# Sliding-window attention with a squared-ReLU feed-forward: two pairs of x, and whole q and k matrices, transposed by DMA

## The chip, the cores and the metric

The kernel runs on one core of one Trainium2 chip. The metric is the time of one execution on the device, in microseconds. Before the change it is 294.82 us (median of 3 runs, 294.8 to 296.04).

## What is computed

Attention over 8 batches, 8 heads, 576 positions and a head size of 64: each position sees itself and the 63 before it. The result, 4608 tokens of 512 values, goes through a feed-forward layer with the square of a ReLU.

```python
scores = np.matmul(q, k.transpose(0, 1, 3, 2)) / np.sqrt(D)
rel = pos[:, None] - pos[None, :]
attn = softmax(np.where((rel >= 0) & (rel < 64), scores, -1e9))
x = np.matmul(attn, v).transpose(0, 2, 1, 3).reshape(4608, 512)
h = np.maximum(x @ w_in, 0.0)          # 512 -> 2048
out = (h * h) @ w_out                  # 2048 -> 512
```

Inputs and output are float32; the products run on float16 copies.

## The kernel before, in words

The tokens are cut into nine blocks of 512. Blocks 0 to 7 hold the first 512 positions of a batch each; block 8 holds the last 64 positions of all batches and needs two k matrices (`k`, `k2`). A block has four pairs of heads (`hp` 0 to 3).

What happens to a block, by the function names in the code:

- **Load and cast.** `load_part` (line 193) loads q, k and v of a block in four pieces of 128 x 512 each from SyncE's queue, `cast_part` (206) makes float16 copies on GpSimd. The float32 pieces live in a ring of ten (`stp`), the float16 pieces of q and k in six buffers each (`p16p`, line 46). Blocks 0 to 2 are loaded by pairs of heads instead (`load_qk_pair`, `cast_qk_pair`).
- **Transposition of q and k.** `transpose_part` (225) lets a DMA from SyncE's queue transpose one piece of 128 x 512 into its quarter of `qT` or `kT`. Blocks 0 to 2 do this on TensorE (`T`, 236).
- **Scores.** `Sc` (263) multiplies for one pair of heads and applies the exponential on ScalarE (283); `M` (286) applies the mask on VectorE as a minimum. The probabilities `pm` live in a ring of four tiles.
- **Second product.** `AV` (293) multiplies with v, which has a column for the sum; `N` (310) divides by that sum on VectorE and writes `xs`, the 512 tokens x 128 values of the pair, in float16.
- **Transposition of x.** `X` (319) brings `xs` into `xT` (values on the partitions): four 128x128 transpositions on TensorE (332) into the pair's own PSUM bank, and one copy out of it, on ScalarE for the blocks here (334, shown as line 118 in the profile). Only block 8 uses a DMA transposition of 128 x 512 for each pair (324).
- **First layer.** `F1` (339) does four matmuls of 512 columns for one of 16 slices of 128 features; VectorE applies the ReLU (349), ScalarE the square (350). For block 8 `L1S` does it in seven products of half size.
- **Second layer.** `F2` for the first two blocks, then `L2S` (543), which forms the product from seven half-size products (`product`, 432, eight matmuls of 256 columns each); VectorE and ScalarE add the parts into `osb`, and `store` writes it from SyncE's queue.

The order is written out by hand. Each of the last eight steps (loop at line 800, step n) runs the second layer of block n and the first layer of block n+1 as a list `fill` of about 30 groups, and puts the attention of block n+2 between the groups: for the first two pairs the scores before group 8, masks before groups 11 and 12, `AV` and `N` before group 14, and `X` of the two pairs before groups 16 and 17; the other two pairs follow 11 groups later (lines 856 to 863; steps 1 and 2 differ by a few groups). Before each group `next_part` (732) is called as often as a quota says; each call issues one load and one cast, and one transposition of q or k whose load lies at least four parts back. SyncE works through its queue in this order: a DMA that waits for a cast holds up the loads and stores behind it.

Every engine takes its instructions in order. SyncE issues DMAs only, and its DMAs share eight completion counters in turn, so each waits for the eighth before it.

Of the kernel before, what the change touches and what calls it, by code (L numbers as in the profile page):

```python
# [9 lines left out]
FP16 = mybir.dt.float16  # L10
# [5 lines left out]
def kernel(  # L16
# [13 lines left out]
    nc = tc.nc  # L30
    B, H, S, D = q.shape
    NT, DM = out.shape
    DFF = moe_w_in.shape[1]
    P = 128
    HP = H // 2
    NBLK = B + 1
# [6 lines left out]

    const = ctx.enter_context(tc.tile_pool(name="const", bufs=1))
    stp = ctx.enter_context(tc.tile_pool(name="stp", bufs=10))
    p16p = ctx.enter_context(tc.tile_pool(name="p16p", bufs=6))
    vpool = ctx.enter_context(tc.tile_pool(name="vpool", bufs=2))
    tpool = ctx.enter_context(tc.tile_pool(name="tpool", bufs=5))
    apool = ctx.enter_context(tc.tile_pool(name="apool", bufs=2))
# [53 lines left out]
    st = {}  # L103
# [12 lines left out]
    def copy(engine, out, in_):  # L116
        if engine is nc.scalar:
            engine.activation(out=out, in_=in_, func=AF.Copy, scale=1.0)  # L118
        else:
            engine.tensor_copy(out=out, in_=in_)  # L120
# [23 lines left out]
        copy(engine, w_out_sb[:, f, :], st["w_out", f][:])  # L144


    p16 = {}
    ev, od, qT, kT = {}, {}, {}, {}

    def new_v(g, half=0):  # L150
        ev[g, half] = vpool.tile([P, 4, H, VW], FP16, name="v_ev", tag="ev", bufs=3)
        nc.gpsimd.memset(ev[g, half][:, :, :, D:VW], 1.0 / X_SCALE)
        if g < B:
            od[g] = vpool.tile([P, 3, H, VW], FP16, name="v_od", tag="od", bufs=2)
            nc.gpsimd.memset(od[g][:, :, :, D:VW], 1.0 / X_SCALE)

    def load_qk_pair(g, what, hp, queue=nc.sync):
        src = {"q": q, "k": k}[what]  # L160
        queue.dma_start(
            out=piece(what, g, hp)[:].rearrange("p (h x) -> p h x", h=2),
            in_=src[g, pair(hp), 0:512, :].rearrange("h (p i) d -> p h (i d)", i=4))
# [6 lines left out]
                in_=v[g, 2 * hp + hh, 0:512, :].rearrange("(c p) d -> p c d", p=P))  # L170

    def cast_qk_pair(g, what, hp, engine):
        t = p16p.tile([P, 512], FP16, name=f"{what}16", tag=f"{what}16")
        p16[what, g, hp] = t
        copy(engine, t[:].rearrange("p (i h d) -> p h i d", i=4, h=2),
             st[what, g, hp][:].rearrange("p (h i d) -> p h i d", i=4, h=2))

    def cast_v_pair(g, hp, engine):
# [27 lines left out]
    def cast_part(g, what, c):  # L206
        if what[0] == "v":
            half = 1 if what == "v2" else 0
            if (g, half) not in ev:
                new_v(g, half)  # L210
            copy(nc.gpsimd, ev[g, half][:, c, :, 0:D],
                 st[what, g, c][:].rearrange("p (h d) -> p h d", h=H))
            return
        t = p16p.tile([P, 512], FP16, name=f"{what}16", tag=f"{what[0]}16")
        p16[what, g, c] = t
        copy(nc.gpsimd, t[:], st[what, g, c][:])

    def shift_v_parts(g):
        for m in range(3):
# [5 lines left out]
    def transpose_part(g, what, c):  # L225
        to = {"q": qT, "k": kT, "k2": kT}[what]
        key = (g, 1 if what == "k2" else 0)
        if key not in to:
            to[key] = tpool.tile([P, HP, 512], FP16, name=f"{what}T", tag="T")
        nc.sync.dma_start_transpose(out=to[key][:, :, c * P:(c + 1) * P], in_=p16[what, g, c][:])  # L230


    pm, av, xs, xT = {}, {}, {}, {}
    at_ps = [ps_at.tile([P, 2, 512], FP32, name=f"at{i}") for i in range(2)]

    def T(g, hp, pool=ps_tr, tag="tr", engine=nc.scalar, own=None):
# [73 lines left out]
    def N(g, hp):  # L310
        a = av[g, hp][:, :, 0:4 * VW].rearrange("p h (j e) -> p h j e", e=VW)
        rden = apool.tile([P, 2, 4], FP32, name="rden", tag="rden")
        nc.vector.reciprocal(out=rden[:], in_=a[:, :, :, D])
        x = apool.tile([P, 4, 2, D], FP16, name="xs", tag="xs", bufs=3)
        xs[g, hp] = x
        nc.vector.tensor_tensor(out=x[:].rearrange("p j h d -> p h j d"), in0=a[:, :, :, 0:D],  # L316
                                in1=rden[:].unsqueeze(3).broadcast_to([P, 2, 4, D]), op=ALU.mult)

    def X(g, hp, engine=nc.scalar, pool=ps_tr, tag="tr", own=None):

        if g not in xT:
            xT[g] = xtpool.tile([P, DMC, 512], FP16, name="xT", tag="xT")
        if g == B:
            nc.sync.dma_start_transpose(out=xT[g][:, hp, :].rearrange("p (j t) -> p j t", j=4),
                                        in_=xs[g, hp][:].rearrange("p j h d -> p (j h d)"))
            return
        if own is not None:
            tr = at_ps[own][:, 0, :].bitcast(FP16).rearrange("p (a b) -> p a b", a=2)
        else:
            tr = pool.tile([P, 2, 512], FP16, name="xtr", tag=tag)  # L330
        for jp in range(4):
            nc.tensor.transpose(out=tr[:, 0, jp * P:(jp + 1) * P], in_=xs[g, hp][:, jp, :, :],  # L332
                                identity=ident[:])
        copy(engine, xT[g][:, hp, :], tr[:, 0, :])
# [265 lines left out]

    ORDER = (1, 2, 6, 5, 7, 3, 4)

    seq = list(range(NBLK))
    PARTS = {g: ("q", "k", "v") for g in range(B)}
    PARTS[B] = ("q", "k", "k2", "v", "v2")

    with tc.manual_schedule():
# [21 lines left out]
        new_v(g0)  # L629
        dve, pool, act = nc.vector, nc.gpsimd, nc.scalar  # L630
        cast_qk_pair(g0, "q", 0, dve)
        cast_qk_pair(g0, "k", 0, dve)
        cast_qk_pair(g0, "q", 1, pool)
        cast_qk_pair(g0, "k", 1, dve)
        cast_qk_pair(g0, "q", 2, pool)
# [20 lines left out]
        cast_v_pair(g0, 2, dve)  # L656
        AV(g0, 0)
        N(g0, 0)
        AV(g0, 1, 0)
        N(g0, 1)  # L660
        cast_v_pair(g0, 3, act)
        add_mask(g0, 3, True)
        Sc(g0, 3, True)
        AV(g0, 2)
        N(g0, 2)
        X(g0, 0)
        X(g0, 1, act, ps_f2, "f2")
        AV(g0, 3, 0)
        N(g0, 3)
        X(g0, 2)  # L670
        for i in range(4):
            for c in range(DMC):
# [59 lines left out]
        def next_part():  # L732

            if parts_left:
                g, w, c = parts_left.pop(0)
                load_part(g, w, c)
                cast_part(g, w, c)
                if w[0] != "v":
                    pending.append((g, w, c))
                elif g < B and c == 3:  # L740
                    shift_v_parts(g)
                behind = len(load_list) - len(parts_left) - 1
            else:
                behind = len(load_list) + 99
            while pending and behind - load_list.index(pending[0]) >= 4:
                transpose_part(*pending.pop(0))
# [53 lines left out]
        for n in range(1, NBLK):  # L800
            g = seq[n]
# [26 lines left out]
            a, b = iter(first), iter(second)  # L828
# [86 lines left out]
```

## Time and profile before

| | |
|---|---|
| median of 3 runs | 294.82 us |
| the profiled execution | 296.1 us |
| its span, first to last instruction | 294.3 us |
| granted TensorE clock | 1.0 |
| TensorE matmuls busy | 284.0 us (96%) |
| VectorE, ScalarE, GpSimd busy | 225.8, 176.8, 128.8 us |
| DMA transpositions of q, k, k2 from SyncE | 24, 24, 4 |
| of x from SyncE (block 8) | 4 |
| 128x128 transpositions of x on TensorE | 128 |

A row of the order of time has the start in us from the span's start, the duration, the engine, the line, the operation, the tiles written and read, and the shape; "x4" is a run of equal instructions, whose duration reaches from the first start to the last end. SPq is SyncE's queue: its durations are those of issuing, and "to landing" counts from the issue to the last byte. Matmuls are pipelined, so one instruction's duration is longer than the distance between two starts. A group's row has the count, the busy time and the mean ns of one, and then the idle time ahead of it and what ended it.

### The profile page before, as it was taken

How to read it: one execution, taken by the hardware profiler on the slowest of the kernel's cores; microseconds unless marked ns; L12 is line 12 of the kernel's file. 1: busy time of each engine (PE TensorE's matmuls, PEld its weight loads, DVE VectorE, ACT ScalarE, POOL GpSimd, SP SyncE). 2: the span in 40 equal slices, each digit the busy share in tenths (PEclk: the TensorE clock that was granted, in tenths of full speed). 3: DMA queues.
4: the chain of work that ended last, by engine and by line, in shares of the span. 5: the costliest groups of instructions: out<-in, count | busy, mean ns of one | idle time of the engine just before them, and what ended most of it. 6: DMA issues, size and time to landing. Idle time of an engine off the chain costs nothing.

```text
span 294.3 us, 7488 instructions
## 1 busy us (share of the span) xinstructions
PE 284.0 (96%) x2945; PEld 183.9 (62%) x2945; DVE 225.8 (77%) x396; ACT 176.8 (60%) x306; POOL 128.8 (44%) x216
## 2 busy tenths in 40 slices
PE   6789999999999999999999999999999999999994
PEld 5444445554445466667666766666666666888883
DVE  4868628698866887888769877987798889878781
ACT  3657847687376556565665566556564655687821
POOL 5778859955583366339226723832342000000002
PEclk9999999999999999999999999999999999999999
DMA  7999999979999998999899999899997024201015
GB/s 231 274 368 392 404 289 282 269 156 195 198 273 199 212 215 144 202 218 195 175 208 234 197 164 233 156 193 207 209 209 204 2 37 92 89 3 73 0 73 143
DMA packets 142627, 56.07 MB, mean 190 GB/s; under 512 B 127712, under 2 KB 134112, under 8 KB 142592
## 3 DMA queue, kind: packets, MB, share of 16 engines
q1 hardware_dynamic: 141120, 53.95, 85.8%
q10 hardware_dynamic: 1328, 1.25, 1.3%
q0 software_dynamic: 144, 0.39, 0.6%
q8 instruction: 23, 0.38, 0.6%
q14 instruction: 12, 0.10, 0.1%
HBM read 38.80 MB, written 9.44 MB: 164 GB/s over the span
## 4 chain that ended last, share of the span: by engine, by line
PE 91%; DMA 4%; SPq 1%; DVE 1%; ACT 1%; issue 0%; POOL 0%; DVEq 0%
PE hps L346 36%; PE chain L434 14%; PE side L434 12%; PE ops L382 5%; PE at L306 4%; PE at L468 4%; PE at L276 3%; PE side L382 2%; PE chain L382 2%; DMA hsum<-in_v_dram 2%; DMA w_st<-in_moe_w_in_dram 2%; PE more L434 2%; PE at L332 2%; PE at L434 1%; PE tr L245 1%; SPq L168 1%
## 5 line engine op out<-in xcount | busy, mean ns | idle before, releaser
L350 ACT ACTIVATE h<-hr 128x512 f16<-128x512 f32 x128 | 80.0, 630 | 78.6 <-DVE hr L349 78.6
L346 PE MATMUL hps<-xT,w_in_sb 128*128 128x512 f16 x496 | 122.5, 379 | 0.3 <-DVE hr L349 0.3
L349 DVE TENSOR_SCALAR hr<-hps 128x512 f32<-128x512 f32 x127 | 85.7, 686 | 32.0 <-PE hps L346 29.7
L346 PEld LDWEIGHTS <-w_in_sb 128*128 128x128 f16 x500 | 46.6, 98 | 42.6 <-issue 1.2
L434 PEld LDWEIGHTS <-hsum 128*128 128x128 f16 x448 | 43.0, 98 | 11.8
L120 POOL CAST v_ev<-st_v 128x512 f16<-128x512 f32 x29 | 22.2, 766 | 42.9 <-DMA st_v<-in_v_dram 42.9
L120 POOL CAST k<-st_k 128x512 f16<-128x512 f32 x33 | 23.0, 701 | 34.2 <-DMA st_k<-in_k_dram 31.6
L434 PEld LDWEIGHTS <-h 128*128 128x128 f16 x336 | 32.7, 98 | 8.5 <-issue 0.8
L283 ACT ACTIVATE pm<-at 128x1024 f16<-128x1024 f32 x35 | 34.1, 1013 | 4.0 <-PE at L276 4.0
L375 POOL DMA_DIRECT2D out_dram<-osb x3 | 1.8, 594 | 63.1 <-ACT osb L550 61.7
L316 DVE TENSOR_TENSOR xs<-at,rden 128x512 f16<-128x512 f32 x36 | 24.9, 691 | 1.2
L290 DVE TENSOR_TENSOR pm<-pm,mask 128x1024 f16<-128x1024 f16 x32 | 23.9, 759 | 1.9 <-ACT pm L283 1.9
L410 DVE TENSOR_TENSOR hsum<-h 128x1024 f16<-128x1024 f16 x28 | 21.0, 750 | 5.2 <-ACT h L350 5.0
L434 PE MATMUL chain<-wsum,hsum 128*128 128x256 f16 x192 | 24.9, 273 | 0.0
L221 POOL CAST v_od<-st_v 64x512 f16<-64x512 f32 x30 | 21.3, 711 | 1.6
L120 POOL CAST q<-st_q 128x512 f16<-128x512 f32 x25 | 17.5, 721 | 6.6 <-DMA st_q<-in_q_dram 6.3
L382 PEld LDWEIGHTS <-h 128*128 128x128 f16 x128 | 11.6, 98 | 12.2
L118 ACT ACTIVATE xT<-at 128x512 f16<-128x512 f16 x22 | 12.8, 586 | 4.0 <-PE at L332 4.0
L306 PEld LDWEIGHTS <-pm 128*64 128x64 f16 x576 | 11.2, 110 | 6.2 <-DVE pm L290 2.3
L382 PE MATMUL ops<-w_out_sb,h 128*128 128x512 f16 x64 | 14.8, 380 | 0.0
L306 PE MATMUL at<-v_ev,pm 128*64 128x65 f16 x384 | 14.1, 198 | 0.4 <-ACT pm L283 0.3
L550 ACT ACTIVATE osb<-chain 128x256 f32<-128x256 f32 x36 | 13.3, 371 | 0.3 <-PE chain L434 0.3
(124 smaller groups left out, 384.7 us busy)
## 6 DMA issues: line engine op xcount, KB each, us to landing
st_k<-in_k_dram SPq DMA_DIRECT2D x32, 256.0 KB, 3.7
out_dram<-osb SPq DMA_DIRECT2D x32, 256.0 KB, 2.9
st_v<-in_v_dram SPq DMA_DIRECT2D x28, 256.0 KB, 4.3
st_q<-in_q_dram SPq DMA_DIRECT2D x24, 256.0 KB, 4.8
w_st<-in_moe_w_in_dram SPq DMA_DIRECT2D x4, 512.0 KB, 6.8
wsum<-in_moe_w_in_dram SPq DMA_DIRECT2D x4, 512.0 KB, 9.7
hsum<-in_moe_w_out_dram SPq DMA_DIRECT2D x4, 512.0 KB, 8.1
wsum<-in_moe_w_out_dram SPq DMA_DIRECT2D x4, 512.0 KB, 9.2
```

What stands on the lines that cost most here:

```text
L120: engine.tensor_copy(out=out, in_=in_)
L221: nc.gpsimd.tensor_copy(out=od[g][to:to + 64, m, :, 0:D], in_=st["v", g, c][of:of + 64, :].rearrange("p (h d) -> p h d", h=H))
L283: nc.scalar.activation(out=p[:, hh, :] if apart else p[:], in_=sc[hh] if apart else both[:], func=AF.Exp, scale=1.0 / float(D) ** 0.5)
L290: nc.vector.tensor_tensor(out=p[:], in0=p[:], in1=m.unsqueeze(1).broadcast_to([P, 2, 512]), op=ALU.min)
L306: nc.tensor.matmul(a[jj * 64:(jj + 1) * 64, hh, jp * VW:jp * VW + D + 1], pm[g, hp][:, hh, j * 64:(j + 1) * 64], vsel, start=True, stop=True)
L316: nc.vector.tensor_tensor(out=x[:].rearrange("p j h d -> p h j d"), in0=a[:, :, :, 0:D], in1=rden[:].unsqueeze(3).broadcast_to([P, 2, 4, D ...
L346: nc.tensor.matmul(hps[:], w_in_sb[:, c, f * P:(f + 1) * P], xT[g][:, c, :], start=(c == 0), stop=(c == DMC - 1))
L349: nc.vector.tensor_scalar(out=hr[:], in0=hps[:], scalar1=0.0, scalar2=None, op0=ALU.max)
L350: nc.scalar.activation(out=h2[g][:, f, :], in_=hr[:], func=AF.Square)
L382: nc.tensor.matmul(f2[g, ts][:], h2[g][:, f, ts * P:(ts + 1) * P], w_out_sb[:, f, :], start=(f == 0), stop=(f == FFC - 1))
L410: (engine or nc.vector).tensor_tensor(out=out, in0=a, in1=b, op=op)
L434: nc.tensor.matmul(to, a[:, f, :], b[:, f, :], start=start and f == 0, stop=f == HF - 1, skip_group_check=True)
```

## The change

For blocks 4 to 7, `N` writes x of the first two pairs into one tile of 128 x 1024 (from the ring of `pm`), and after the second pair one DMA from SyncE's queue transposes it into two quarters of `xT`; `X` of these pairs has no work on TensorE and ScalarE any more. For blocks 5 to 8, the four float16 pieces of q, and of k (and k2), lie in one tile, written by GpSimd in strips of 128, and one DMA transposes 128 x 2048 after the fourth piece, at the place where that piece's transposition stood. The float16 pieces of all blocks now come from one ring of three tiles of four pieces.

```diff
-    p16p = ctx.enter_context(tc.tile_pool(name="p16p", bufs=6))
+    p16p = ctx.enter_context(tc.tile_pool(name="p16p", bufs=3))
...
+    def whole(g):
+        return g in seq[5:]
+
+    def tile16(what, g, c):
+        if c == 0:
+            all16[what, g] = p16p.tile([P, 4, 512], FP16, name=f"{what}16", tag="16")
+        p16[what, g, c] = all16[what, g][:, c, :]
+        return p16[what, g, c]
...
-        t = p16p.tile([P, 512], FP16, name=f"{what}16", tag=f"{what[0]}16")
-        p16[what, g, c] = t
-        copy(nc.gpsimd, t[:], st[what, g, c][:])
+        t = tile16(what, g, c)
+        if whole(g):
+            t = all16[what, g][:].rearrange("p a (c d) -> p a c d", c=4)[:, :, c, :]
+            copy(nc.gpsimd, t, st[what, g, c][:].rearrange("p (a d) -> p a d", a=HP))
+        else:
+            copy(nc.gpsimd, t, st[what, g, c][:])
...
-        nc.sync.dma_start_transpose(out=to[key][:, :, c * P:(c + 1) * P], in_=p16[what, g, c][:])
+        if not whole(g):
+            nc.sync.dma_start_transpose(out=to[key][:, :, c * P:(c + 1) * P], in_=p16[what, g, c])
+        elif c == 3:
+            nc.sync.dma_start_transpose(out=to[key][:].rearrange("p a (c t) -> p (a c) t", c=4),
+                                        in_=all16[what, g][:].rearrange("p a e -> p (a e)"))
...
+    XDMA = [(g, 0) for g in (4, 5, 6, 7)]
...
-        x = apool.tile([P, 4, 2, D], FP16, name="xs", tag="xs", bufs=3)
-        xs[g, hp] = x
+        if (g, hp // 2) not in XDMA:
+            x = xs[g, hp] = apool.tile([P, 4, 2, D], FP16, name="xs", tag="xs", bufs=3)[:]
+        else:
+            if hp % 2 == 0:
+                pair_x[g] = apool.tile([P, 2, 4, 2, D], FP16, name="xs2", tag="pm", bufs=4)
+            x = xs[g, hp] = pair_x[g][:, hp % 2, :, :, :]
...
+        if (g, hp // 2) in XDMA:
+            if hp % 2 == 1:
+                nc.sync.dma_start_transpose(out=xT[g][:, hp - 1:hp + 1, :].rearrange("p a (j t) -> p (a j) t", j=4),
+                                            in_=pair_x[g][:].rearrange("p a j h d -> p (a j h d)"))
             return
```

`cast_qk_pair` takes its tiles from `tile16` in the same way.

More of the change, by code (lines that the diff above doesn't have):

```diff
@@ L144, in cast_w_out @@
         copy(engine, w_out_sb[:, f, :], st["w_out", f][:])
-    p16 = {}
+    seq = list(range(NBLK))
+    p16, all16 = {}, {}
     ev, od, qT, kT = {}, {}, {}, {}
@@ L172, in cast_qk_pair @@
     def cast_qk_pair(g, what, hp, engine):
-        t = p16p.tile([P, 512], FP16, name=f"{what}16", tag=f"{what}16")
-        p16[what, g, hp] = t
-        copy(engine, t[:].rearrange("p (i h d) -> p h i d", i=4, h=2),
+        t = tile16(what, g, hp)
+        copy(engine, t.rearrange("p (i h d) -> p h i d", i=4, h=2),
              st[what, g, hp][:].rearrange("p (h i d) -> p h i d", i=4, h=2))
@@ L229, in transpose_part @@
             to[key] = tpool.tile([P, HP, 512], FP16, name=f"{what}T", tag="T")
-        nc.sync.dma_start_transpose(out=to[key][:, :, c * P:(c + 1) * P], in_=p16[what, g, c][:])
-    pm, av, xs, xT = {}, {}, {}, {}
+        if not whole(g):
[3 more added lines that the diff above has]
+                                        in_=all16[what, g][:].rearrange("p a e -> p (a e)"))
+    pm, av, xs, pair_x, xT = {}, {}, {}, {}, {}
+    XDMA = [(g, 0) for g in (4, 5, 6, 7)]
     at_ps = [ps_at.tile([P, 2, 512], FP32, name=f"at{i}") for i in range(2)]
@@ L313, in N @@
         nc.vector.reciprocal(out=rden[:], in_=a[:, :, :, D])
-        x = apool.tile([P, 4, 2, D], FP16, name="xs", tag="xs", bufs=3)
-        xs[g, hp] = x
-        nc.vector.tensor_tensor(out=x[:].rearrange("p j h d -> p h j d"), in0=a[:, :, :, 0:D],
+        if (g, hp // 2) not in XDMA:
[4 more added lines that the diff above has]
+            x = xs[g, hp] = pair_x[g][:, hp % 2, :, :, :]
+        nc.vector.tensor_tensor(out=x.rearrange("p j h d -> p h j d"), in0=a[:, :, :, 0:D],
                                 in1=rden[:].unsqueeze(3).broadcast_to([P, 2, 4, D]), op=ALU.mult)
@@ L324, in X @@
             nc.sync.dma_start_transpose(out=xT[g][:, hp, :].rearrange("p (j t) -> p j t", j=4),
-                                        in_=xs[g, hp][:].rearrange("p j h d -> p (j h d)"))
+                                        in_=xs[g, hp].rearrange("p j h d -> p (j h d)"))
+            return
+        if (g, hp // 2) in XDMA:
+            if hp % 2 == 1:
+                nc.sync.dma_start_transpose(out=xT[g][:, hp - 1:hp + 1, :].rearrange("p a (j t) -> p (a j) t", j=4),
+                                            in_=pair_x[g][:].rearrange("p a j h d -> p (a j h d)"))
             return
@@ L601 @@
     ORDER = (1, 2, 6, 5, 7, 3, 4)
-    seq = list(range(NBLK))
     PARTS = {g: ("q", "k", "v") for g in range(B)}
```

## The prediction

> **What bounds the kernel now.** I read the page's first four parts, then busy time by stretch, then the order of time on TensorE and on SP around the edits. The whole first:
>
> ```profile
> span 294.3 us, 7488 instructions
> PE 284.0 (96%) x2945; PEld 183.9 (62%) x2945; DVE 225.8 (77%) x396; ACT 176.8 (60%) x306; POOL 128.8 (44%) x216
> ...
> PE   6789999999999999999999999999999999999994
> ...
> PEclk9999999999999999999999999999999999999999
> ...
> PE 91%; DMA 4%; SPq 1%; DVE 1%; ACT 1%; issue 0%; POOL 0%; DVEq 0%
> ```
>
> TensorE is full in all slices but the first and the last few us, at the full granted clock, and 91% of the chain that ended last is its own work. An average can hide a stage with another limit, so the stretches in which the changed blocks lie (us; busy time of each engine, granted clock, DMA share, GB/s):
>
> ```profile
> 103.50:133.50 30.00, 30.00 (x322) 19.84 (x321) 24.60 (x42) 18.51 (x34) 15.74 (x25) 1.00 1.07 198
> 193.00:223.00 30.00, 29.98 (x321) 19.99 (x319) 24.27 (x44) 17.30 (x33) 9.85 (x15) 1.00 1.21 203
> ...
> 250.00:294.30 44.30, 40.16 (x359) 34.78 (x357) 31.16 (x58) 25.48 (x52) 1.78 (x3) 1.00 0.21 64
> ```
>
> In the first two, TensorE works 30.00 of 30 us; VectorE is next with 24.6, ScalarE has 18.5. Only behind 250 us, where nothing is edited, does TensorE idle (4.1 us). So an instruction taken from TensorE between 120 and 211 us should move everything behind it forward by what it held the stream, and one taken from another engine should give nothing by itself. The DMA share above 1 says that queues of packets overlap there: the DMA side is loaded, and I have to ask whether it becomes the bound.
>
> **The change, part by part.**
>
> *x of two pairs leaves TensorE.* For blocks 4, 5, 6 and 7 two groups of four 128x128 transpositions (line 332) and two evictions on ScalarE go. In a pipelined engine the duration of one instruction is not its price; the price is how far the next start is pushed. Block 4 and block 7 (start, us, ...):
>
> ```profile
> 120.78 0.39 PE L332 MATMUL at<-ident,xs 128*128 128x128 f16 x4
> 121.00 1.03 PE L346 MATMUL hps<-xT,w_in_sb 128*128 128x512 f16 x4
> 121.86 0.39 PE L332 MATMUL at<-ident,xs 128*128 128x128 f16 x4
> 122.09 1.04 PE L434 MATMUL side<-w_out_sb,h 128*128 128x256 f16 x8
> ...
> 209.31 0.39 PE L332 MATMUL at<-ident,xs 128*128 128x128 f16 x4
> 209.54 1.04 PE L434 MATMUL chain<-w_out_sb,h 128*128 128x256 f16 x8
> 210.41 0.39 PE L332 MATMUL at<-ident,xs 128*128 128x128 f16 x4
> 210.63 1.03 PE L346 MATMUL hps<-xT,w_in_sb 128*128 128x512 f16 x4
> ...
> L332 PE MATMUL at<-ident,xs 128*128 128x128 f16 x88 | 8.5, 219 | 0.0
> ```
>
> From a group's start to the next start are 0.22, 0.23, 0.23 and 0.22 us, though the group is shown as 0.39 us and one instruction as 219 ns. Eight groups at 0.225 us are **1.8 us**, all on the chain. The Trainium skill (TensorE: Matmul & The Clock Gate, "Part 4: PE-mode transpose") gives about 275 ns for a 128x128 transposition inside a kernel. By that the 32 transpositions would be worth 8.8 us; the trace disagrees, at 0.225 us for four. I keep it as a rival below.
>
> The two evictions per block (586 ns each by the row below) go from ScalarE, which nothing waits for here: I cost them at nothing. What was covered by X before is next in line: the first-layer matmuls, which wait for the bank that VectorE empties. Their waits are 0.3 us in the whole run, so no cover is lost.
>
> ```profile
> L118 ACT ACTIVATE xT<-at 128x512 f16<-128x512 f16 x22 | 12.8, 586 | 4.0 <-PE at L332 4.0
> L346 PE MATMUL hps<-xT,w_in_sb 128*128 128x512 f16 x496 | 122.5, 379 | 0.3 <-DVE hr L349 0.3
> ```
>
> *What SP's queue gets and loses.* Twelve transpositions of 128x512 become three for block 8 (q, k, k2), and eight become two for blocks 5, 6 and 7; four transpositions of 128x1024 for x are added. The rows of SP: q and k (min, median, max ns of the issue), then x of block 8 with its time to landing, a load, the next transposition, two stores:
>
> ```profile
> L230 SPq DMA_TRANSPOSE qT<-q x24: 1191/1220/2391, 61.6 to 196.1; - x24
> DMA to landing us min/median/max: 2.7/3.6/5.5
> ...
> L324 SPq DMA_TRANSPOSE xT<-xs x4: 1191/1210/1242, 239.7 to 249.4; - x4
> DMA to landing us min/median/max: 2.4/2.4/4.4
> ...
> 120.99 0.57 SPq L197 DMA_DIRECT2D st_v<-in_v_dram  x1
> 121.67 1.21 SPq L230 DMA_TRANSPOSE kT<-k  x1
> ...
> 129.35 1.00 SPq L371 DMA_DIRECT2D out_dram<-osb  x2
> ```
>
> No row shows a transposition of more than 512 columns. If one issue were one push whatever the size, it would take 1.2 us; if it is made of the same pieces, four times as much, 4.9 us, and 2.4 us for x. I take the upper end, since 2048 columns are four times the work of the nearest row; both ends stay in the range. SP's work for one block is now 12 x 0.57 + 8 x 1.22 + 2 x 1.00 = 18.6 us, and with 0.1 us between its 24 rows 21 us. With the change it is 6.8 + 2 x 4.9 + 2.4 + 2.0 = 21.0, and about 1.9 between 19 rows: 22.9 us at the upper end, about 14.3 at the lower. A block takes (209.31 - 120.78) / 3 = 29.5 us. The queue has room either way.
>
> *Later results.* A merged transposition starts when the last of its four casts is done; the first three pieces lose their lead, but the products need all four anyway. The last piece of k is the one that counts (block 5, then k2 of block 8), against the first scores that read it:
>
> ```profile
> 127.81 1.45 SPq L230 DMA_TRANSPOSE kT<-k  x1
> 215.02 1.39 SPq L230 DMA_TRANSPOSE k2T<-k  x1
> ...
> 141.41 0.64 PE L276 MATMUL at<-qT,kT 64*128 64x64 f16 x32
> 232.08 0.29 PE L276 MATMUL at<-qT,kT 64*128 64x64 f16 x8
> ```
>
> With 3.6 us from issue to landing that is 131.4 against 141.4, and 218.6 against 232.1: 10 and 13 us to spare. In the changed order SP issues for block 5 four loads of k, q's transposition, three loads of v, x of block 4, a load, then k's. q's can start when its four casts are done:
>
> ```profile
> 112.36 2.74 POOL L120 CAST q<-st_q 128x512 f16<-128x512 f32 x4
> ```
>
> From 115.1 go 4.9 for q, 4 x 0.67 for the loads and 2.4 for x, so k's starts near 125.1 and lands 4.9 + (3.6 - 1.2) later, at 132.4: 9 us early. Behind both stand v's loads and the stores, which wait with them; v is first read in the same block's second products, six groups behind the scores, so it has at least the same reserve. The DMA side itself gets only x on top, 0.26 MB for a block in which 198 GB/s x 29.5 us = 5.8 MB move, 4%; and since the reserve grows from block 5 to block 8, the transfers are not what falls behind now.
>
> x of a block waits on SP for VectorE's second x (done just ahead of 121.86 in block 4), and blocks loads behind it for at most that long. Its readers are the next step's first-layer matmuls:
>
> ```profile
> 134.37 1.03 PE L346 MATMUL hps<-xT,w_in_sb 128*128 128x512 f16 x4
> 223.99 1.15 PE L346 MATMUL hps<-xT,w_in_sb 128*128 128x512 f16 x4
> ...
> 216.46 3.29 SPq L204 DMA_DIRECT2D st_v<-in_v_dram  x4
> ```
>
> Block 4: issued near 122, landed by about 127 (2.4 for the issue, at most 2.4 behind it), read at 134.4. Block 7 is the tight one: it stands in the middle of the four loads that begin at 216.46, so it is issued near 217.5, lands near 222.3 at the latest and is read at 224.0 less the 1.8 us gained. The reserve is nearly nil at this upper end, and a few us if SP is ahead by the work it saves. I cost it at nothing, at most 1 us.
>
> *Buffers and casts.* The 16-bit pieces now share three buffers of four pieces. A cast into a reused buffer waits for all four transpositions of the old one. The two places where this could bite are block 2's k behind block 1's last transposition, and block 3's k behind block 2's:
>
> ```profile
> 44.90 0.39 PE L245 MATMUL at<-ident,k 128*128 128x128 f16 x4
> 67.01 0.39 PE L245 MATMUL tr<-ident,k 128*128 128x128 f16 x4
> ...
> 49.59 0.61 POOL L120 CAST k<-hsum 128x512 f16<-128x512 f32 x1
> 68.29 2.19 POOL L120 CAST k<-st_k 128x512 f16<-128x512 f32 x3
> ```
>
> Both casts already start after them (49.6 behind 45.3, 68.3 behind 67.4): nothing. Block 5 and later: GpSimd writes four strips of 128 instead of 512 in a row; the nearest rows are its casts in pieces of 64 (the next row, 766 ns) and the plain ones at 0.61 us, so up to 0.16 us each on an engine that is idle half the time: nothing on the path.
>
> ```profile
> L120 POOL CAST v_ev<-st_v 128x512 f16<-128x512 f32 x29 | 22.2, 766 | 42.9 <-DMA st_v<-in_v_dram 42.9
> ```
>
> x's pair takes a turn in the ring of four that holds the probabilities; who comes round to it is the next block's second Exp, behind the scores at 141.4 for block 5, 14 us after x landed: nothing.
>
> **Sum.** 1.8 us from TensorE, nothing else on the path. The profiled execution took 296.1 us, 1.8 around its span of 294.3; it should become 294.3. The median shown is 294.82, 1.3 below that execution, and the same 1.8 us makes it **293.0**.
>
> **Rivals.**
>
> *The gain is swallowed.* TensorE's stream gets denser, and the next wait takes over: that of the second products for VectorE's mask, the largest on TensorE in these blocks.
>
> ```profile
> PEld L306 <- DVE pm L290: 2.3, 7, 0.4
> ```
>
> For it: each group gone leaves VectorE 0.22 us less between the first-layer results that it has to empty before it comes to the next mask. Against it: VectorE has over 5 us free in each stretch. If half to all is given back, 293.9 to 294.8.
>
> *SP's queue becomes the bound: slower.* The mechanism is the size of a merged issue. With x at half of q's price, the queue fills a block's 29.5 us when 2.5 T + 6.8 + 2.0 + 1.9 = 29.5, so from T = 7.5 us on, 1.9 us for each 512 columns against 1.22 now. At twice the present price (T = 9.8) each block runs 5.7 us late; four blocks make 23, less the 13 us in hand at block 8: TensorE waits about 10 us, 303. For it: no row of this width, and a loaded DMA side. Against it: no row of a plain single is near it (medians 1.21 and 1.22). The Trainium skill (VectorE: DVE Perf Modes, "The three transpose paths" and its rules) speaks against this part of the change: TensorE for 128x128 where PSUM will do, with 390 ns against 1309 ns by DMA. By that, 32 blocks would cost 29 us more, were they on the path; the trace has 1.21 us for four blocks on a queue that nothing waits for.
>
> *A larger gain by the price of single transpositions.* If each cost TensorE its 219 ns, 32 x 0.219 = 7.0 us would go, giving 287.8. The starts above exclude it nearly.
>
> That the change does not do what it says I leave out: the built order has the eight groups gone and one transposition for each matrix of blocks 5 to 8.
>
> **How the numbers follow.** Forecast 293.0, within 292.4 and 293.6: chance 0.66. Swallowed, up to 294.8: 0.20. SP the bound, 296 to 303: 0.13. Larger gain: 0.01. The range 292.4 to 294.9 holds the first two; it reaches beyond the late block 7 (293.0 + 1 us) too. A measurement of this kernel tells about 0.5% from no change, 1.5 us: faster means under 293.35, which is most of the forecast (0.58) and the larger gain; 0.08 of the forecast and all of the swallowed gain fall within it. Faster 0.59, same 0.28, slower 0.13.
>
> **What would show it.** Right: 56 instead of 88 in the group of x's transpositions on TensorE, a block period near 29.1 us, no wait of TensorE for a DMA, SP's merged issues at or under 4.9 us and 2.4 us for x. Swallowed: more idle time ahead of the second products. Wrong: weight loads of the scores or of the first layer that wait for DMA, from the block at which the queue falls behind.

## The result

The changed kernel takes 293.88 us (median of 22 runs, 293.06 to 296.38), the kernel before 295.33 beside it (median of 22, 294.5 to 296.04). The ratio is 0.9957, with a 95% interval of 0.9943 to 0.9971: 1.3 us less (0.9 to 1.7). A second comparison, in later runs, gave 0.9932 (0.9908 to 0.9956), 2.0 us less (1.3 to 2.7). Both agree between 1.3 and 1.7 us. The forecast was 1.8 us, to 293.0.

The page of the changed kernel, its first lines and its chain; the profiled execution took 293.76 us.

```profile
span 291.7 us, 7363 instructions
PE 282.2 (97%) x2913; PEld 182.3 (62%) x2913; DVE 224.5 (77%) x396; ACT 173.2 (59%) x298; POOL 124.2 (43%) x216
...
PE 90%; DMA 4%; SPq 1%; DVE 1%; ACT 1%; issue 0%; POOL 0%; DVEq 0%; ACTq 0%
```

Against before, TensorE has 32 instructions fewer and is busy 1.8 us less, ScalarE 3.6 us less, and TensorE still makes up the chain. The two stretches in which TensorE was full are still full (span, busy time of PE, PEld, DVE, ACT, POOL, clock, DMA share, GB/s):

```profile
103.50:133.50 30.00, 30.00 (x317) 19.86 (x316) 25.20 (x43) 17.81 (x33) 19.65 (x29) 1.00 1.18 224
193.00:223.00 30.00, 30.00 (x319) 19.97 (x317) 24.68 (x46) 16.48 (x30) 8.15 (x15) 1.00 1.00 191
```

So what left TensorE was not replaced by a wait there. The groups say the same: 56 transpositions of x instead of 88, no idle time ahead of the first layer, and 2.7 us of waiting for VectorE's mask ahead of the second products' weight loads, where before had 2.3.

```profile
L372 PE MATMUL hps<-xT,w_in_sb 128*128 128x512 f16 x496 | 122.4, 379 | 0.0
L323 PEld LDWEIGHTS <-pm 128*64 128x64 f16 x576 | 11.2, 110 | 6.2 <-DVE pm L307 2.7 <-issue 1.6 <-DVE hr L375 0.4
L358 PE MATMUL at<-ident,xs 128*128 128x128 f16 x56 | 5.4, 219 | 0.0
```

At block 4, where before has a group of transpositions ahead of each product, the order of time on TensorE now has the products alone, 0.87 us from start to start:

```profile
119.44 1.04 PE L460 MATMUL chain<-w_out_sb,h 128*128 128x256 f16 x8
120.31 1.03 PE L372 MATMUL hps<-xT,w_in_sb 128*128 128x512 f16 x4
121.17 1.04 PE L460 MATMUL side<-w_out_sb,h 128*128 128x256 f16 x8
```

**Where the time went** shows best against fixed points of the work. TensorE's scores mark them: the first of blocks 3 and 4, the last pairs' of block 7 and of block 8. First before, then the changed kernel (start, us, ...):

```profile
82.85 0.64 PE L276 MATMUL at<-qT,kT 64*128 64x64 f16 x32
112.51 0.64 PE L276 MATMUL at<-qT,kT 64*128 64x64 f16 x32
212.47 0.64 PE L276 MATMUL at<-qT,kT 64*128 64x64 f16 x32
240.44 0.29 PE L276 MATMUL at<-qT,kT 64*128 64x64 f16 x8
```

```profile
82.36 0.64 PE L293 MATMUL at<-qT,kT 64*128 64x64 f16 x32
112.01 0.64 PE L293 MATMUL at<-qT,kT 64*128 64x64 f16 x32
210.25 0.64 PE L293 MATMUL at<-qT,kT 64*128 64x64 f16 x32
237.89 0.29 PE L293 MATMUL at<-qT,kT 64*128 64x64 f16 x8
```

From block 4's mark to block 7's, the stretch that holds all eight edited groups of x, before takes 99.96 us and the changed kernel 98.24: 1.72 less, of 8 x 0.225 = 1.80. Behind it 0.33 us more are gained up to block 8's mark, and the first two marks lie 0.5 us earlier. Two profiles of one kernel can differ by nearly as much there: in a second one of before the first mark lies at 82.49, 0.36 earlier. I trust the stretch, not the ends.

SyncE's queue in the changed kernel: first the merged transpositions of q and of k, then x's of 128 x 1024 with its summary of landing; then single rows in order of time.

```profile
L245 SPq DMA_TRANSPOSE qT<-q x4: 2894/3264/4321, 114.0 to 189.1; - x4
...
L245 SPq DMA_TRANSPOSE kT<-k x4: 3016/3787/4400, 122.4 to 195.6; - x4
...
L350 SPq DMA_TRANSPOSE xT<-xs x4: 1233/1342/2902, 120.5 to 209.6; - x4
...
DMA to landing us min/median/max: 3.4/4.2/5.2
```

```profile
120.47 1.23 SPq L350 DMA_TRANSPOSE xT<-xs  x1
...
122.43 3.02 SPq L245 DMA_TRANSPOSE kT<-k  x1
...
204.73 3.52 SPq L245 DMA_TRANSPOSE k2T<-k  x1
...
209.62 2.90 SPq L350 DMA_TRANSPOSE xT<-xs  x1
```

A merged issue takes 2.9 to 4.4 us, less than four single ones (4 x 1.22). The queue reaches x of block 7 at 209.62, 8 us ahead of the 217.5 that the prediction read from before's order. The matrix lands by 214.8, and the first layer reads it at 221.6.

### The profile page after: what moved, and what is told of

Same layout as the page of the kernel before. It is cut to its first block, busy times and chain, and to the rows that moved or that the text cites. A ratio compares the mean times of both kernels' runs of the same rounds, so it can differ in the third digit from the quotient of the medians.

```text
span 291.7 us, 7363 instructions
## 1 busy us (share of the span) xinstructions
PE 282.2 (97%) x2913; PEld 182.3 (62%) x2913; DVE 224.5 (77%) x396; ACT 173.2 (59%) x298; POOL 124.2 (43%) x216
## 4 chain that ended last, share of the span: by engine, by line
PE 90%; DMA 4%; SPq 1%; DVE 1%; ACT 1%; issue 0%; POOL 0%; DVEq 0%; ACTq 0%
PE hps L372 37%; PE chain L460 15%; PE side L460 12%; PE ops L408 4%; PE at L494 4%; PE at L323 3%; PE at L293 3%; PE side L408 2%; PE chain L408 2%; DMA w_st<-in_moe_w_in_dram 2%; PE more L460 2%; DMA hsum<-in_v_dram 2%; PE at L460 1%; PE at L358 1%; PE tr L262 1%; SPq L178 1%
## 5 line engine op out<-in xcount | busy, mean ns | idle before, releaser
L120 POOL CAST v_ev<-st_v 128x512 f16<-128x512 f32 x29 | 19.3, 666 | 44.1 <-DMA st_v<-in_v_dram 44.1
L120 POOL CAST k<-st_k 128x512 f16<-128x512 f32 x33 | 20.5, 625 | 28.5 <-DMA st_k<-in_k_dram 24.2
L233 POOL CAST v_od<-st_v 64x512 f16<-64x512 f32 x30 | 23.0, 768 | 1.7
L436 DVE TENSOR_TENSOR hsum<-h 128x1024 f16<-128x1024 f16 x28 | 19.7, 705 | 4.9 <-ACT h L376 4.8
L120 POOL CAST q<-st_q 128x512 f16<-128x512 f32 x25 | 16.7, 680 | 12.2 <-DMA st_q<-in_q_dram 11.6
L460 PE MATMUL side<-wsum,hsum 128*128 128x256 f16 x104 | 13.5, 273 | 0.0
```

The source lines that it names most:

```text
L233: nc.gpsimd.tensor_copy(out=od[g][to:to + 64, m, :, 0:D], in_=st["v", g, c][of:of + 64, :].rearrange("p (h d) -> p h d", h=H))
L436: (engine or nc.vector).tensor_tensor(out=out, in0=a, in1=b, op=op)
L460: nc.tensor.matmul(to, a[:, f, :], b[:, f, :], start=start and f == 0, stop=f == HF - 1, skip_group_check=True)
```

## The experiments

The first theory is the prediction's own: the gain is TensorE's price of the eight groups, the queue has room for x, and the merged transpositions are worth nothing by themselves. Against it stands that one of the two parts cannot do without the other, or gives something of its own. Each run names its own rivals.

**x by DMA without the merges.** In the changed kernel:

```diff
     def whole(g):
-        return g in seq[5:]
+        return False
```

> x of the first two pairs of blocks 4 to 7 by DMA as in the change; q and k of all blocks piece by piece as before. Theory (the gain is TensorE's stream: eight groups at 0.225 us; SP's queue has room): 1.8 us under before, or 0.8 under if x of block 7 comes late behind the 44 single pieces, at most 1 us of wait in all. Rival (the merged q and k pay, by a shorter queue on SP): not faster than before, within 0.5 us, or slower if x fills the queue.

Measured: 301.33 us, ratio to before 1.0179 (1.0158 to 1.0200), 5.3 us slower. So x alone is not a gain but a loss: the theory is out, and the rival in which x fills the queue holds. What TensorE waited for (us in total, times, longest):

```profile
PE hps L372 <- DMA xT<-xs: 3.7, 2, 3.3
```

The order of time on SyncE, at block 5's first transposition of q, at x of block 4, behind block 6's loads of q, and at x of blocks 6 and 7:

```profile
107.84 1.03 SPq L206 DMA_DIRECT2D st_k<-in_k_dram  x1
112.57 1.19 SPq L243 DMA_TRANSPOSE qT<-q  x1
...
127.84 1.26 SPq L350 DMA_TRANSPOSE xT<-xs  x1
...
136.10 1.37 SPq L206 DMA_DIRECT2D st_k<-in_k_dram  x1
140.49 1.19 SPq L243 DMA_TRANSPOSE qT<-q  x1
141.73 0.58 SPq L206 DMA_DIRECT2D st_k<-in_k_dram  x1
...
188.37 1.74 SPq L350 DMA_TRANSPOSE xT<-xs  x1
...
220.15 1.95 SPq L350 DMA_TRANSPOSE xT<-xs  x1
```

And TensorE at the start of block 7's first layer, with its idle time and releaser in brackets, then its busy time and granted clock (before the DMA share) in stretches of 3 us:

```profile
221.49 1.04 PE L460 MATMUL chain<-wsum,h 128*128 128x256 f16 x8
225.86 1.89 PE L372 MATMUL hps<-xT,w_in_sb 128*128 128x512 f16 x4 [3.33 <-DMA xT<-xs]
227.54 1.92 PE L460 MATMUL chain<-w_out_sb,h 128*128 128x256 f16 x8
```

```profile
225.00:228.00 3.00, 2.14 (x7) 0.50 1.28 258
228.00:231.00 3.00, 3.00 (x12) 0.50 0.73 279
231.00:234.00 3.00, 3.00 (x22) 0.88 0.00 0
```

x of block 7 is issued 10.5 us later than in the changed kernel. Most of that lag is there at x of block 4 already, 7.4 us (127.84 against 120.47); at blocks 5 to 7 it is 7.1, 9.2 and 10.5. Three reasons can be read in the rows. A single transposition of q stands between two loads of k and waits for its cast: SyncE does nothing from 108.9 to 112.6, and again from 137.5 to 140.5, and three more loads of k wait behind it each time. In the changed kernel all four loads of k go ahead of the merged one. Three of k's four transpositions stand ahead of x of block 4, where the merged one follows it. And the issues themselves add up: from x of block 6 to x of block 7 SyncE issues almost without a pause for 31.8 us, longer than a block, because 16 loads and all 12 transpositions of block 8, with its two k matrices, stand there. What each of the three is worth was not measured; the second standstill did not make the lag grow, since from x of block 4 to x of block 5 30.4 us pass here and 30.6 in the changed kernel.

TensorE then waits 3.3 us, and pays again: for 6 us the granted clock is 0.50, and the groups start 1.7 us apart instead of 0.87. The Trainium skill (TensorE: Matmul & The Clock Gate, "Why this matters for your kernels") warns of idle gaps of more than about 3 us between bursts of matmuls, after which the clock falls back to half; this row agrees. (In the run with merges in block 8 only, below, an idle time of 2.74 us was followed by a lower clock as well, 0.73 and 0.70 in the same stretches of 3 us: somewhat less than 3 us was enough.) Four groups at half clock cost about 2.9 us (from 225.86 to 232.20, where the fifth starts, is 6.34, less 4 x 0.87). With the waits of 3.7 that is 6.6, less 1.8 for the groups gone 4.8, within the interval of 4.7 to 5.9.

**The merges without x by DMA.**

```diff
-    XDMA = [(g, 0) for g in (4, 5, 6, 7)]
+    XDMA = []
```

> q and k of blocks 5 to 8 by one DMA per matrix as in the change; x of all pairs of blocks 4 to 7 on TensorE as before. Theory: within 0.3 us of before, since nothing waits for the queue. Rival (the merge pays): 1.3 us under before, the whole measured gain. Second rival (the merge costs something and so explains why 1.3 us and not 1.8 were measured): 0.5 us over before.

Measured: 295.03 us, ratio 0.9970 (0.9957 to 0.9983), 0.9 us faster. The prediction had the merges at nothing, and that is outside the interval; the 1.3 us of the first rival is at its other edge (0.5 to 1.3). A second run and the traces of both follow below.

**All pairs of blocks 4 to 7 by DMA.** The second pairs too, at their old places (the joint tile of x is kept for each two pairs then):

```diff
-    XDMA = [(g, 0) for g in (4, 5, 6, 7)]
+    XDMA = [(g, h) for g in (4, 5, 6, 7) for h in (0, 1)]
```

> The change, with the other two pairs of blocks 4 to 7 by DMA as well, at the places where TensorE transposed them. Theory: sixteen groups fewer, 3.6 us, but these DMAs are issued about 2 us before the next step's first layer reads them and land 4.2 us after the issue (median of x in the changed kernel), so TensorE waits 2 to 3 us at the start of four steps: 4 to 8 us over before. Rival (landing is hidden anyway): 3.6 us under before.

Measured: 305.31 us, ratio 1.0314 (1.0292 to 1.0336), 9.3 us slower; more than was expected. It waits for x four times:

```profile
PE hps L372 <- DMA xT<-xs: 9.2, 4, 4.3
```

**All pairs, with the second pairs three groups earlier.** The same list of pairs, and in the order written by hand:

```diff
-            for i, two in zip((11, 22) if n == 1 else (9, 20) if n == 2 else (9, 17) if n == 6 else (8, 19),
+            for i, two in zip((11, 22) if n == 1 else (9, 17) if n in (2, 6) else (8, 16),
...
-                        put(i + (7 if u[0] == B else 8 + t), lambda u=u, t=t: X(*u, own=t))
+                        put(i + (7 if u[0] == B or (u[0], u[1] // 2) in XDMA else 8 + t), lambda u=u, t=t: X(*u, own=t))
```

> As the run before, but the scores of the second two pairs stand before group 16 (17 in step 2), and x's DMA right behind its sums: five groups more between issue and reading. Theory: no wait, sixteen groups at 0.225 us: 3.6 us under before, twice the change's own sum. Rival (the gain is swallowed by waits for VectorE in a denser stream): no more than the change alone, 1.3 us under before.

Measured: 297.14 us, ratio 1.0056 (1.0030 to 1.0082), 1.7 us slower. Both expectations missed. x is nearly in time (1.0 us of waits for it in all), but the second products now stand closer to their masks. The waits of TensorE's products, then of its weight loads:

```profile
PE at L323 <- DVE pm L307: 3.3, 3, 1.4
```

```profile
PEld L323 <- DVE pm L307: 6.4, 12, 1.5
```

Sixteen groups at 0.225 us left TensorE, 3.6 us, and more came back: a gain swallowed by waits for VectorE, as in the prediction's first rival, but met in a version that moves the masks' readers.

**Before once more, for its profile.** The kernel before, unchanged.

> The kernel before, unchanged, for a second profile. In the first one the first scores of block 3 start at 82.85 us; in the five profiles with edits at 81.6 to 82.4, though nothing that they run ahead of that was meant to be faster. Theory (the first profile of before had a late start): 82.0 to 82.5, and a span of 293.5 to 294.0. Rival (the ring of three buffers makes the start faster): 82.8 again.

Measured: 295.67 us, span 294.0. The first scores of block 3 start at 82.49, at the late end of what the theory allowed; so the first profile's start was late by no more than some 0.4 us, and the stretch from block 4's mark to block 7's is 99.94 us (112.15 to 212.09), as it was (99.96).

**The ring of three tiles alone.** Both edits of the first two experiments at once: no merges, x on TensorE, only the shared ring is left of the change.

> Of the change, only the ring of three buffers of four pieces; q and k piece by piece, x on TensorE. Theory 1 (the 0.9 us of the run with merged q and k alone comes from the ring, in the first 80 us): 0.9 us under before. Theory 2 (it comes from the merged transpositions themselves): within 0.3 us of before.

Measured: 295.54 us, ratio 1.0000 (0.9982 to 1.0018). The buffers cost and give nothing, so what the merges gave is not the ring's.

**Each of the eight groups three times.** In the kernel before, 16 groups added:

```diff
-        for jp in range(4):
-            nc.tensor.transpose(out=tr[:, 0, jp * P:(jp + 1) * P], in_=xs[g, hp][:, jp, :, :],
-                                identity=ident[:])
+        for again in range(3 if g in (4, 5, 6, 7) and hp < 2 else 1):
+            for jp in range(4):
+                nc.tensor.transpose(out=tr[:, 0, jp * P:(jp + 1) * P], in_=xs[g, hp][:, jp, :, :],
+                                    identity=ident[:])
```

> The kernel before, with the transpositions of the eight groups that the change takes away done three times each: sixteen groups of four more on TensorE, same results. Theory (a group holds the stream for 0.225 us): 3.6 us over before. Rival (each instruction costs its 219 ns): 14 us over. Second rival (a group costs less, and so the gain came out at 1.3 us instead of 1.8): 2.6 us over.

Measured: 298.75 us, ratio 1.0109 (1.0080 to 1.0138), 3.2 us slower (2.4 to 4.1), 0.20 us for a group. TensorE's order of time at block 4:

```profile
121.19 0.83 PE L333 MATMUL at<-ident,xs 128*128 128x128 f16 x12
121.86 1.03 PE L347 MATMUL hps<-xT,w_in_sb 128*128 128x512 f16 x4
```

Twelve transpositions hold the stream for 0.67 us, 0.056 us each. The price by single durations, 219 ns, would have made the kernel 14 us slower; it is excluded. The expected 3.6 us and the second rival's 2.6 both lie within the interval, so the time does not tell them apart.

**x by DMA, merged in block 8 only.** In the changed kernel `return g in seq[8:]`.

> x of the first two pairs by DMA as in the change, but one DMA per matrix only for block 8's q, k and k2; blocks 5 to 7 piece by piece. Theory (what x alone lacked was that the queue comes to x of block 7 in time; the three merges ahead of it save the time that is needed): no wait over 0.5 us at block 7, so 1.0 to 1.8 us under before, like the whole change. Rival (the lead is lost in blocks 5 to 7 already): block 7's first layer waits 2 us or more again and the time is over before.

Measured: 299.67 us (runs from 297.4 to 301.9), ratio 1.0122 (1.0081 to 1.0163), 3.6 us slower. The theory, that the three merges around x of block 7 are enough, fails: x of block 4 is issued at 128.31 and x of block 7 at 220.69, as late as without any merge, and TensorE waits for it:

```profile
226.20 1.76 PE L372 MATMUL hps<-xT,w_in_sb 128*128 128x512 f16 x4 [2.74 <-DMA xT<-xs]
```

**The counterpart: merged in blocks 5, 6 and 7 only.** `return g in seq[5:8]`, run together with the next three.

> x by DMA as in the changed kernel, q and k merged in blocks 5, 6 and 7 only; block 8's q, k and k2 piecewise again. If the lead of SyncE's queue at x of block 7 comes from the merges of blocks 5 to 7, x of block 7 is issued near 210 to 213, TensorE does not wait for it, and the time is that of the changed kernel, within 0.5 us. Rival (block 8's merges, which stand around x of block 7 in the queue, matter too): x of block 7 is issued near 215 to 217, lands near 221, and TensorE waits 0 to 1 us; up to 1.5 us slower than the changed kernel.

Measured: 294.37 us, ratio 0.9956 (0.9938 to 0.9975), the changed kernel's 293.91 in the same comparison being 0.9932 (0.9908 to 0.9956). No wait of TensorE for x. On SyncE:

```profile
210.14 3.10 SPq L350 DMA_TRANSPOSE xT<-xs  x1
```

x of block 7 is issued 0.5 us behind the changed kernel's 209.62, and the time is 0.5 us over the changed kernel's by the medians, the most that was expected. The six merges of blocks 5 to 7 are enough to keep the queue ahead, and together with the run before this shows that they are needed; block 8's are not.

**The changed kernel again, and the merges alone again, side by side.**

> The changed kernel once more, beside merges alone in the same runs, so that what x adds to the merges is read from one comparison. Theory (eight groups of x at 0.225 us come off TensorE, nothing else on the path): this kernel is 1.8 us faster than merges alone. Rival (part of it is given back, as the two earlier ratios, 0.9957 and 0.9970, suggest): 0.4 us, under 0.8. Against the kernel before: 0.9943 to 0.9971 again.

> Merged transpositions of q and k, x of all pairs on TensorE as before. Theory (the merges touch no TensorE work, so they are worth nothing by themselves; the 0.9970 of the first run was of its chip or an accident): 0.998 to 1.002 of the kernel before. Rival (they are worth 0.9 us by themselves): 0.9957 to 0.9983 again.

Measured: the changed kernel 293.91 us, the merges alone 294.85, before 295.69; ratios 0.9932 (0.9908 to 0.9956) and 0.9973 (0.9952 to 0.9994). For the merges 0.9973 lies within the rival's range and under the theory's 0.998 to 1.002, whose edge the interval still reaches; the first run had left it out. By the medians x adds 0.9 us to the merges. The two half-widths together (0.0024 and 0.0021, as the root of the sum of squares) leave some 0.3 to 2.1 us around the 1.2 of the ratios, so the times do not tell 1.8 from 0.4. The traces do. The marks of the merges alone, all four in this second run, then the same in the first:

```profile
81.88 0.64 PE L293 MATMUL at<-qT,kT 64*128 64x64 f16 x32
111.54 0.64 PE L293 MATMUL at<-qT,kT 64*128 64x64 f16 x32
211.62 0.64 PE L293 MATMUL at<-qT,kT 64*128 64x64 f16 x32
239.20 0.29 PE L293 MATMUL at<-qT,kT 64*128 64x64 f16 x8
```

```profile
81.63 0.64 PE L293 MATMUL at<-qT,kT 64*128 64x64 f16 x32
111.32 0.64 PE L293 MATMUL at<-qT,kT 64*128 64x64 f16 x32
211.31 0.64 PE L293 MATMUL at<-qT,kT 64*128 64x64 f16 x32
239.66 0.29 PE L293 MATMUL at<-qT,kT 64*128 64x64 f16 x8
```

The marks of blocks 4 and 7 in all profiles in which TensorE's products do not wait for x (us; "block 3 too" is the next experiment):

| kernel | block 4 | block 7 | between |
|---|---|---|---|
| before, two profiles | 112.51, 112.15 | 212.47, 212.09 | 99.96, 99.94 |
| ring alone | 111.97 | 211.98 | 100.01 |
| merges alone, two profiles | 111.32, 111.54 | 211.31, 211.62 | 99.99, 100.08 |
| changed, two profiles | 112.01, 112.47 | 210.25, 211.07 | 98.24, 98.60 |
| merged in blocks 5 to 7 only | 111.49 | 209.54 | 98.05 |
| block 3 too | 111.60 | 209.91 | 98.31 |
| eight groups three times | 112.92 | 216.32 | 103.40 |

With x of the eight groups on TensorE the stretch takes 99.94 to 100.08 us, with x by DMA 98.05 to 98.60, on the means 1.7 less; sixteen groups more make it 3.4 longer. Both are 0.21 us for a group. So in the stretch the merges give nothing, and x gives all of the gain.

The 0.8 to 0.9 us of the merges alone lie outside it. In the two profiles the first mark is 0.9 and 0.6 us earlier than in before's second one, but that is ahead of any merged transposition: the first is issued at 115.5 and 114.2. From block 7's mark to block 8's 28.35 and 27.58 us pass, where before has 27.97: one slower, one faster. So the traces show no part of the kernel in which the merges gain; where their 0.8 to 0.9 us come from stays open.

**Block 3 too.** `whole` from block 3 on, and x of block 3's first two pairs by DMA:

```diff
-        return g in seq[5:]
+        return g in seq[3:]
...
-    XDMA = [(g, 0) for g in (4, 5, 6, 7)]
+    XDMA = [(g, 0) for g in (3, 4, 5, 6, 7)]
```

> The changed kernel with block 3 taken in: x of its first two pairs by DMA too, and q and k merged in blocks 3 and 4 as well. Theory: two more groups at 0.225 us come off TensorE, 0.45 us faster than the changed kernel, 1.8 us faster than before at the measured gain, if no DMA is late. Rival: merged transpositions of blocks 3 and 4 wait for their last cast while the queue is still behind the loads of the start, and a score or x of block 3 is late by 1 to 4 us: 0.5 to 3.5 us slower than the changed kernel.

Measured: 293.98 us, ratio 0.9944 (0.9927 to 0.9960). TensorE's products wait for no DMA. Block 3's two groups lie between the first mark and block 4's, and there 29.25 us pass (82.35 to 111.60), 0.40 less than the changed kernel's 29.65, where 0.45 was expected. The rival is out, and the time cannot be told from the changed kernel's. No version tried beats it measurably.

## Why the prediction was right, and where its reasons were not

**TensorE's term was right.** 0.225 us for a group of four, 1.8 us in all: 1.7 us are missing in the stretch on the mean of four profiles (1.72 and 1.36 in the changed kernel's two), and tripled groups cost 0.20 us each by the times, 0.21 by the stretch and 0.22 by the starts. The larger gain by single prices is excluded by the tripled groups.

**The total gain was taken a little too large.** Over the whole execution the gain is 1.3 us (0.9 to 1.7) and 2.0 (1.3 to 2.7) in the two comparisons; the first leaves the forecast of 1.8 out. 293.88 lies 0.3 above the 292.4 to 293.6 that the prediction gave its own sum, in the part of the range that it gave to the swallowed gain, and not under the 293.35 that it called faster. Of the 0.9 us to 293.0, 0.5 is the kernel before, 295.33 in the comparison instead of 294.82, and the rest is the gain, 1.45 by the medians.

**ScalarE at nothing was right.** ScalarE has 3.6 us less to do, and no waiting moved with it; the first layer's waits went from 0.3 us to 0.0 (0.3 again in the second profile).

**The size of a merged issue was taken too high, harmlessly.** For q and k 4.9 us was taken, the upper end, and 2.9 to 4.4 were measured. For x 2.4 was taken; the median is 1.34, but the last one, at block 7, took 2.90, over that end, and landed after 5.2 us instead of 4.8. The rival in which a merged issue of 7.5 us and more makes the queue the bound is refuted in its size.

**"The queue has room either way" is the step that failed as a reason.** The sum of 21.0 us for a block counted issues and gaps of 12 loads and 8 transpositions. It did not count the time in which the queue stands still with a transposition that waits for its cast, nor loads that wait behind it, nor that block 8 has 24 loads and 12 transpositions, most of them ahead of x of block 7. With single pieces SyncE needs 30.4, 30.2 and 31.8 us from one x to the next, more than the 29.5 of a block. At the upper end the prediction also had the merges at no relief in issue time, 2 x 4.9 for 8 x 1.22; with them x of block 7 is issued 10.5 us earlier. Without them it is 3.3 us late. The reserve was nearly nil at the place that the prediction named as the tight one, and its cost of "nothing, at most 1 us" holds only because the merges come with it. With x alone the same step would have been wrong by 7 us (1.8 faster expected, 5.3 slower measured).

**Buffers at nothing was right** (1.0000). **The swallowed gain** is not seen in the changed kernel: the mask waits of the weight loads are 2.7 and 3.0 us in its two profiles, 2.3 and 3.2 in before's, and 3.6 in the second profile of the merges alone, where no group has left, so they do not follow the groups. That the mechanism exists is seen where the second products were moved towards their masks.

**By DMA or by TensorE:** the rule of the Trainium skill that the prediction weighed (VectorE: DVE Perf Modes, "The three transpose paths" and "Rules for kernel authors") prefers TensorE for 128x128, at 390 ns against 1309. Here eight such blocks take 1.34 us of SyncE's issue time (median) and 0.45 us of TensorE's. The slower path wins because nothing waits for it, and loses by 5.3 us as soon as something does.

That the total came so close is in part luck: the times of the merges alone show 0.8 to 0.9 us that the prediction does not have, and whose place was not found. With it the parts add up to 2.6 us, more than the first comparison allows.

## What to carry to other kernels

Price an instruction on a pipelined engine by the distance of the starts around it, and check the price by repeating it. Before moving work to a queue that looks half empty, count its fullest stretch and not the average one, and the time in which its head waits for another engine, since everything behind it waits too; grouping four small transfers into one also moves three of them out of the way of what stands behind them. A late transfer at a full TensorE costs more than the wait, because the clock falls as well: 3.7 us of waits made the kernel 7.1 us slower than the groups that left would have it (5.3 + 1.8), 9.2 us of waits 12.9 (9.3 + 3.6).

## What the runs showed of the hardware

In the changed kernel a DMA transposition of 128x2048 inside SBUF takes 2.9 to 4.4 us to issue, of 128x1024 1.2 to 2.9 (median 1.34), of 128x512 1.2 (median): issue time grows less than the size. An idle time of TensorE of 3.3 us is followed by about 6 us at a granted clock of 0.50, one of 2.7 us by 6 us at 0.73 and 0.70. In the run with all pairs at their old places, the two waits of 4.1 and 4.3 us were followed by the same kind of dip (busy time and granted clock, in stretches around the first and the third of the four), the two of about 0.4 us by none (granted clock 1.00):

```profile
136.00:140.00 4.00, 2.46 (x11) 0.75 1.27 233
140.00:145.00 5.00, 5.00 (x30) 0.86 1.30 250
...
202.00:206.00 4.00, 3.90 (x16) 0.60 1.28 225
```
